# A third fold of the column Fourier transform in an attention and Fourier-mixing kernel, with new step priorities

## The chip, the cores and the metric

The kernel runs on one core of one Trainium2 chip. The metric is the time of one execution on the device, in microseconds (us). Before the change the median of three runs was 578.76 us (578.48 to 579.12). The profile is one execution taken by the hardware profiler. Its lines name the engines: PE (TensorE, the matrix unit; PEld is its weight load), DVE (VectorE), ACT (ScalarE), POOL (GpSimd) and SP (which issues DMAs). L1051 is line 1051 of the kernel before.

## The reference: what is computed

Eight batches of 12 heads, 448 tokens and 64 columns per head go through cosine attention. The result, 448 tokens by 768 columns, goes through the real part of a two-dimensional Fourier transform, a normalisation and a two-layer network:

```python
q_n = q / (norm(q) + 1e-6); k_n = k / (norm(k) + 1e-6)
attn = softmax(q_n @ k_n.T / tau)
x = attn @ v                               # heads side by side: (8, 448, 768)
u = x + real(fft(fft(x, axis=1), axis=2))  # tokens, then columns
un = (u - mean(u)) / sqrt(var(u) + 1e-6)
out = u + relu(un @ w_ch1) @ w_ch2         # 768 -> 3072 -> 768
```

## The kernel before, in words

All steps are put into a list by `Plan.add`: an operation with its name, its engine or the engines that may take it, an estimated duration, a priority, and what it reads and writes. `Plan.schedule` then deals the operations out to the five engines, earliest possible start first and the lower priority number among equals. The result is a fixed order for each engine, which executes its list strictly in that order with semaphore waits between engines. `SHIFT` is a table of corrections, by operation name and occurrence, that are added to the priorities before the scheduling. It holds 335 numbers. So a change in `SHIFT` changes no operation, but it can change the order on each engine and, where two engines are allowed, the engine. `Plan.fill` finally puts short dummy matmuls ("warm" steps, L1571, six matmuls of 128 columns each) where the planner expects PE to be idle.

A batch b goes through these steps (the number after the underscore is the batch, the one before it a part):

- `attn`: for the first two batches `first_norm` squares (`sq`, ACT), sums (`ss`, DVE), takes ln and exp (`ln`, `nrm`, ACT) and a reciprocal (`eps`, `rcp`, DVE) for the norms. It scales (`sc`, L704 and L708, DVE or POOL), transposes with matmuls (`tk` L732, `tq` L744 to L746, `tt` L757) and evacuates PSUM (`ek`, `eq`, `et`, L723 and L767). `tq` writes its 128 results to every third PSUM column. Then come the scores (`qk`, L889, L901, L902), the exponentials (`ex`, L867, ACT), the product with v (`pv`, L920 and L926), a reciprocal and a scaling into `X` (`rd`, `x`, L944 and L946). The pairs of heads are taken in the order 0, 1, 2, 3, 5, 4.
- `fold`, called after the last three pairs: the 448 tokens have been split into sums and differences already. `fa` (L963) and `f0`, `f1` (L970) fold the columns once more; for batches 1 to 7 `g` (L992) folds a second time, into an array `G` of 193 columns by four token parts, for even (eo = 0) and odd (eo = 1) frequencies. `g0` writes columns 1 to 127 after pair 5, `g1` columns 128 to 191 after pair 4; `gc` (L1522, L1523) copies columns 0 and 192. Then the token transform `fs0` (L1013, columns 0 to 127) follows `g0` and `fs1` (columns 128 to 192) follows `g1`. Each is 8 matmuls that move 225 columns, and `te` (L1024 on ACT, L1025 on DVE) evacuates each into `Tt`. For batch 0 the first block is done directly from the first fold (L1008).
- `fft`: the column transform `fd0`, `fd1` (L1051) is 8 matmuls each for batches 1 to 7. They move 193 or 192 columns of the table `CSd` and write contiguous PSUM columns 0 to 192 (even) and 193 to 384 (odd). `qe` (L1064), `pq` (L1067) and `u` (L1079) combine the result with `X`; `ba` (L1111), `bs` (L1113), `ln2` (L1116), `rs` (L1118) and `un` (L1120) normalise. For batch 0 `tn` (L1130) transposes with matmuls and `eu` (L1138) evacuates; for the others a DMA transposes (L1141).
- `ffn`: `h` (L1188) is the first layer, `relu` (L1204) its evacuation, `y` and `m` (L1332) the second layer, `fin` (L1352, L1357, L1364) the addition of u and L1378 or L1386 the store. For the last two batches the first layer runs as a fast product of seven multiplications (`p`, L1283). `wsums` and `sums` prepare sums of weights on DVE.

The network of batch b − 1 and the attention of batch b stand interleaved on PE. In the profile's span the first network step of batch 0, `h0_0`, starts at 51.49 us: what lies before it is called the head here, and the rest the body. The loads of q and k for a batch are issued on SP, those of v and of the weights on POOL.

The tables are made in the head: `sins` and `sind` (L568 to L571) fill `CSs` and `CSd` with ACT's sine, which needs the table loads `ldt0`, `ldt1` and `ldt` (L576, L578, L588); `sinn` (L586) negates a table, and `sinp` (L581) another on POOL.

Of the kernel before, what the change touches and what calls it, by code (L numbers as in the profile page):

```python
# [13 lines left out]
DM = H * DH  # L14
# [8 lines left out]
NG = DM // 4 + 1  # L23
ORDER = (0, 1, 2, 3, 5, 4)
# [54 lines left out]
}  # L79

LATE = {r"W[12]_\d+": 1.5, "tmd": 2.0, r"sq\d_2": 4.0, r"sq\d_\d": 2.0, r"sq[KQT]\d_1": 2.0, r"ktd\d": 3.0, r"qdup\d": 3.0, r"qk\d._[2-7]": 1.5, r"pv\d\d_[2-7]": 2.0, r"pv\d\d_1": 1.0, r"h\d+_[1-7]": 0.3}
PIECE = {r"sc[KQ]\d_0": 0.95, r"scT\d_0": 0.42, r"sc\d_\d": 0.6, r"f[avm]\dp_\d": 0.54, r"t\d\d": 0.94}
PORT = r"eps\d|f[a01]\d_\d|g\d_\d|u\d+_\d|un\d_\d|s\d\d_\d|t\d\d|sc[KQT]\d_\d"

# [318 lines left out]
def t_dve(n, mode=1):  # L408
    return 0.1 + n / (960.0 * mode)
# [1222 lines left out]
```

## Time and profile before

| | us |
|---|---|
| median of 3 runs | 578.76 |
| span of the profiled execution, first to last instruction | 576.7 |
| difference between the two | 2.06 |
| PE busy in the span | 562.2 |
| DVE busy | 428.6 |
| ACT busy | 391.4 |
| POOL busy | 210.7 |

A row of the profile's timeline gives the start, the length, the engine, the line, the operation, what it writes and reads, and how often; in square brackets stands how long the engine was idle before it, and who ended that. In the chain of waits the row gives start, length, and engine with tile and line. Matmuls overlap in a pipeline: one takes 0.2 to 0.3 us from start to end, while the next starts much sooner. So the pace of PE is read from starts, not from durations.

### The profile page before, as it was taken

What the parts mean: (1) busy time and instruction counts of PE and PEld (TensorE: products, weight loads), DVE (VectorE), ACT (ScalarE), POOL (GpSimd) and SP (SyncE); (2) the same over time, 40 slices, a digit from 0 to 9 for tenths busy, and PEclk for the clock granted to TensorE, in tenths of its full rate; (3) what the DMA queues carried; (4) which work ended last, traced back from release to release, by engine and by line L of the source; (5) the groups of instructions that cost most, each with busy time, mean ns of one, the idle gap of its engine ahead of it and who ended that gap; (6) DMA issues with size and microseconds to landing.
All of it is one profiled execution on the core that took longest, in us unless ns stands there. A gap on an engine that the chain in (4) does not pass through costs nothing.

```text
span 576.7 us, 15950 instructions
## 1 busy us (share of the span) xinstructions
PE 562.2 (97%) x6496; PEld 443.3 (77%) x6496; DVE 428.6 (74%) x1066; ACT 391.4 (68%) x764; POOL 210.7 (37%) x323
## 2 busy tenths in 40 slices
PE   3999999999999999999999999999999999999998
PEld 3679888686687786978787687778878687969695
DVE  8879888887688778776768568765877587876363
ACT  8898885467975685687747676488737753848170
POOL 8525424543462525523270435413180120031303
PEclk9899999999999999999999999999999999999999
DMA  9999999892597729952594339932592110022001
GB/s 218 186 218 168 167 180 166 177 166 56 119 150 87 177 44 133 174 110 61 110 140 73 66 103 147 162 70 71 106 108 57 28 57 28 3 42 71 27 30 56
DMA packets 187834, 62.19 MB, mean 108 GB/s; under 512 B 166736, under 2 KB 185552, under 8 KB 187760
## 3 DMA queue, kind: packets, MB, share of 16 engines
q1 hardware_dynamic: 129792, 38.35, 35.2%
q0 software_dynamic: 57968, 22.81, 30.8%
q8 instruction: 51, 0.84, 0.6%
q14 instruction: 23, 0.19, 0.1%
HBM read 51.90 MB, written 11.01 MB: 109 GB/s over the span
## 4 chain that ended last, share of the span: by engine, by line
PE 94%; DVE 3%; POOL 2%; issue 1%; POOLq 0%
PE PS L1332 34%; PE PS L1188 31%; PE PS L1283 7%; PE PS L926 6%; PE PS L889 6%; PE PS L1013 2%; PE PS L920 2%; PE PS L1051 2%; PE PS L744 1%; PE PS L1571 1%; PE PS L901 1%; PE PS L902 1%; POOL VB L847 1%; DVE X L946 1%; DVE SM L679 1%
## 5 line engine op out<-in xcount | busy, mean ns | idle before, releaser
L1188 PE MATMUL PS<-UNT,W1b 128*128 128x256 bf16 (+1 forms) x1872 | 187.9, 256 | 0.0
L1188 PEld LDWEIGHTS PS<-UNT,W1b 128*128 128x128 bf16 x1872 | 156.2, 98 | 18.9 <-issue 4.3
L867 ACT ACTIVATE E<-PS 128x900 bf16<-128x900 f32 (+1 forms) x192 | 148.7, 828 | 27.8 <-PE PS L889 25.7
L1332 PE MATMUL PS<-W2b,HQ 128*128 128x384 bf16 x768 | 133.3, 326 | 0.0
L815 POOL TENSOR_TENSOR QH<-STG,SM 128x256 bf16<-128x256 f32 x126 | 79.1, 655 | 82.1 <-DVE SM L624 73.1
L1332 PEld LDWEIGHTS PS<-W2b,HQ 128*128 128x128 bf16 x768 | 73.9, 98 | 45.4 <-issue 0.9
L1357 POOL TENSOR_TENSOR OUTB<-OUTB,U 128x192 f32<-128x192 f32 x66 | 37.9, 594 | 163.6 <-ACT OUTB L1352 163.3
L1204 ACT ACTIVATE HQ<-PS 128x512 bf16<-128x512 f32 x83 | 49.6, 597 | 42.5 <-PE PS L1188 42.1
L1332 PE MATMUL PS<-TX,HQ 128*128 128x384 bf16 (+2 forms) x408 | 71.0, 321 | 0.0
L1427 DVE TENSOR_TENSOR HQ<-HQ 128x512 bf16<-128x512 bf16 x141 | 60.6, 456 | 13.8 <-ACT HQ L1204 7.7
L1332 PEld LDWEIGHTS PS<-TX,HQ 128*128 128x128 bf16 x408 | 38.4, 98 | 23.5 <-issue 1.1
L926 PE MATMUL PS<-VB,E 128*128 128x65 bf16 x1152 | 51.2, 193 | 0.0
L926 PEld LDWEIGHTS PS<-VB,E 128*128 128x128 bf16 x1152 | 47.6, 97 | 1.1
L806 ACT ACTIVATE QH<-STG 128x384 f32<-128x384 f32 x84 | 42.4, 521 | 7.8 <-DVE SM L808 7.1
L808 DVE TENSOR_REDUCE SM<-QH 128x6 f32<-128x384 f32 x84 | 44.2, 539 | 4.3 <-ACT QH L806 3.9
L1204 DVE TENSOR_SCALAR HQ<-PS 128x512 bf16<-128x512 f32 x43 | 29.7, 691 | 21.1 <-PE PS L1188 20.6
L1386 POOL DMA_INDIRECT out_dram<-OUTB,IDX x21 | 22.9, 1092 | 53.2 <-DVE OUTB L1364 36.4
L920 PE MATMUL PS<-VZ,E 128*128 128x130 bf16 x192 | 41.6, 219 | 0.3 <-DVE X L946 0.3
L889 PE MATMUL PS<-QK 64*128 64x225 bf16 x576 | 39.9, 260 | 0.2 <-ACT E L867 0.2
L1079 DVE SCALAR_TENSOR_TENSOR U<-ACG,X 128x384 bf16<-128x384 f32 (+3 forms) x70 | 39.4, 583 | 0.9
L1352 ACT ACTIVATE OUTB<-PS 128x384 f32<-128x384 f32 x33 | 16.2, 492 | 30.4 <-PE PS L1332 30.1
L946 DVE TENSOR_TENSOR X<-PS,RD 128x512 bf16<-128x512 f32 (+1 forms) x49 | 33.1, 678 | 1.2
(177 smaller groups left out, 795.5 us busy)
## 6 DMA issues: line engine op xcount, KB each, us to landing
STG<-in_k_dram SPq DMA_DIRECT2D x18, 384.0 KB, 4.1
STG<-in_q_dram SPq DMA_DIRECT2D x18, 384.0 KB, 3.8
VB<-in_v_dram POOLq DMA_DIRECT2D x24, 192.0 KB, 5.9
W1b<-in_moe_w_ch_dram POOLq DMA_DIRECT2D x12, 384.0 KB, 6.7
W2b<-in_moe_w_ch_dram POOLq DMA_DIRECT2D x12, 384.0 KB, 7.3
out_dram<-OUTB SPq DMA_DIRECT2D x7, 384.0 KB, 4.0
TX<-in_k_dram SPq DMA_DIRECT2D x2, 576.0 KB, 5.6
TX<-in_q_dram SPq DMA_DIRECT2D x2, 576.0 KB, 6.0
```

Source lines behind the costliest of these rows:

```text
L806: P.add("act", lambda a, sq=sq, src=buf[:, w * x:w * x + w]: a.activation(sq, src, ACTF.Square), t_act(w), pr, f"sq{i}_{b}", reads=bn, wri ...
L808: P.add("dve", lambda v, o=SS[:, i, H // ns * x:H // ns * (x + 1)], sq=sq: v.tensor_reduce(o, sq.rearrange("p (h d) -> p h d", d=DH), AX.X ...
L815: r = v.tensor_tensor(v3(qh)[:, h:h + 4], v3(buf)[:, h:h + 4], RN[:, i, h:h + 4].unsqueeze(2).to_broadcast((128, 4, DH)), AluOp.mult)
L867: return a.activation(o, self.PS[:, bk:bk + nc_, 0:SQ2], ACTF.Exp, scale=1.0 / self.tau)
L889: i = pe.matmul(self.PS[:, bk + h, c0:c0 + NK], self.KT[r, jj, kt * 128:(kt + 1) * 128], self.QT[r, jj, cols], start=True, stop=True)
L920: r = pe.matmul(o, st(6), self.VZ[:, j, :], start=not split, stop=(split and i == 0), skip_group_check=True)
L926: r = pe.matmul(o[:, 65 * h:65 * h + 65], st(2 * kt + h), self.VB[:, kt, 2 * j + h, :], start=(split and i == h == kt == 0), stop=((not sp ...
L1188: r = pe.matmul(self.PS[:, bk, x * n:(x + 1) * n], self.W1b[:, j, ft * 128:(ft + 1) * 128], self.UNT[:, j, cs], start=(j == 0), stop=(j == ...
L1204: return e.activation(o, i, ACTF.Relu) if e is self.nc.scalar else e.tensor_relu(o, i)
L1283: r = pe.matmul(o[:, 128 * f:128 * f + 128], lhs(j, n * g + f), rhs[:, j, :], start=(start and j == 0 and f == 0), stop=(stop and j == 2 a ...
L1332: r = pe.matmul(self.PS[:, bk, 0:n], lhs(f), rhs(f), start=(start and f == 0), stop=(stop and f == NF // 2 - 1), skip_group_check=True)
L1427: P.add("dve", lambda v: v.tensor_tensor(cs(o), cs(a), cs(bq), op), 0.46, -0.5, f"{nm}{k}_{b}", reads=rd, writes=hr(o)(k))
```

## The change

Four things change.

1. `fold`, batches 1 to 7: after `g1`, two new DVE operations `e0` and `e1` fold the even half of `G` a third time, about column 96, into two blocks of 97 columns by four parts (`NM = DM // 8 + 1 = 97`). They lie in the memory of `F`, which is free by then.
2. The token transforms `fs0` and `fs1` of batches 1 to 7 both come after the last fold, in a new function `fsum`. For even frequencies they take the folded blocks (97 columns each instead of 128 and 65). The number of matmuls and the 225 columns moved by each stay. The evacuations still wait for the `pv` of pair 5, the last reader of the memory that they write.
3. `fft`, batches 1 to 7: an even matmul of `fd` moves every second column of the table, 97 or 96 instead of 193, and writes every second PSUM column. The odd ones stay at 192. The number of matmuls stays. Column 96 of the fold would be counted twice, so a new step `halfd` halves one row of the table `CSd` once, after the column transform of batch 0.
4. The table `SHIFT` is replaced as a whole: 446 numbers instead of 335, with 123 operation names in both.

The core of the diff (the `SHIFT` tables and unchanged lines are cut):

```diff
+NM = DM // 8 + 1
...
+        if b and blk:
+            E0 = F[:, 0].rearrange("p a c -> p (a c)")[:, 0:8 * NM].rearrange("p (d a c) -> p d a c", d=2, a=4)
+            for i, o in ((0, AluOp.add), (1, AluOp.subtract)):
+                P.add("dve", lambda v, i=i, o=o: v.tensor_tensor(E0[:, i], G[:, 0, :, 0:NM], gp(G[:], [[NG, 4], [-1, NM]], NG - 1), o), t_dve(4 * NM, 2) + 0.03, pj, f"e{i}_{b}",
+                      reads=["G00", "G01", "G10", "G11", "Gc0", "Gc1"], writes=[f"F0{x}" for x in range(3)] if i == 0 else ["Ed"], after=[P.ops[-1]] if i else [])
+        if b == 0:
+            self.fsum(b, blk, m, direct, pj)
+        elif blk:
+            for x in range(2):
+                self.fsum(b, x, (128, NG - 128)[x], False, pj)
+
+    def fsum(self, b, blk, m, direct, pj):
...
             for eo in range(2):
+                mm = NM if b and eo == 0 else m
                 for s in range(2):
-                    o = self.PS[0:m, bk + eo, s * NK:(s + 1) * NK]
+                    o = self.PS[0:mm, bk + eo, s * NK:(s + 1) * NK]
...
                     for t in range(2):
                         k = 128 if t == 0 else RB
-                        r = pe.matmul(o, G[0:k, eo, 2 * s + t, blk * 128:blk * 128 + m],
-                                      self.CSs[0:k, t, s, :], start=(t == 0), stop=(t == 1))
+                        lhs = E0[0:k, blk, 2 * s + t, :] if b and eo == 0 else G[0:k, eo, 2 * s + t, blk * 128:blk * 128 + m]
+                        r = pe.matmul(o, lhs, self.CSs[0:k, t, s, :], start=(t == 0), stop=(t == 1))
...
-                  writes=[...], after=[tile.users[0], self.pvs[-1 if blk == 0 else -2]], tiles=(tile,))
+                  writes=[...], after=[tile.users[0], self.pvs[-1 if b == 0 and blk == 0 else -2]], tiles=(tile,))
...
+                def mul(c, out, s, eo, d, k, tab, start, stop):
+                    o0 = (2 * eo + d) * SQ2 + s * NK + 128 * kt
+                    return pe.matmul(PS[:, c, out], self.Tt[0:k, o0:o0 + 128], tab, start=start, stop=stop, skip_group_check=True)
                 for d in range(2):
                     k = 128 if d == 0 else NG - 128
                     for s in (1, 0):
+                        if b:
+                            par = d ^ s
+                            mul(bk + s, slice(par, NG, 2), s, 0, d, NM, self.CSd[0:NM, 0, s, par:NG:2], d == 0, False)
+                            r = mul(bk + s, slice(NG, NL), s, 1, d, k, self.CSd[0:k, d, s, NG:NL], False, d == 1)
+                            continue
...
+            if b == 0 and kt:
+                row = self.CSd[NM - 1:NM, 0, :, 0:NG]
+                P.add(("dve", "act"), lambda e: e.activation(row, row, ACTF.Copy, scale=0.5) if e is self.nc.scalar else e.tensor_scalar(row, row, 0.5, None, AluOp.mult),
+                      (0.25, 0.5), 100, "halfd", reads=["CSd"], writes=["CSd"], after=self.fd_ops)
```

More of the change, by code (lines that the diff above doesn't have):

```diff
@@ L995, in fold @@
                   writes=[f"G{blk}{i}"])
+        if b and blk:
[9 more added lines that the diff above has]
+    def fsum(self, b, blk, m, direct, pj):
+        P, F, G = self.P, self.F, self.G
+        FP = DM // 2 + 2
+        E0 = F[:, 0].rearrange("p a c -> p (a c)")[:, 0:8 * NM].rearrange("p (d a c) -> p d a c", d=2, a=4)
         tile = Tile("G")
@@ L1012, in fn @@
                         k = 128 if t == 0 else RB
-                        r = pe.matmul(o, G[0:k, eo, 2 * s + t, blk * 128:blk * 128 + m],
-                                      self.CSs[0:k, t, s, :], start=(t == 0), stop=(t == 1))
+                        lhs = E0[0:k, blk, 2 * s + t, :] if b and eo == 0 else G[0:k, eo, 2 * s + t, blk * 128:blk * 128 + m]
+                        r = pe.matmul(o, lhs, self.CSs[0:k, t, s, :], start=(t == 0), stop=(t == 1))
             return r
         P.add("pe", fn, (16 if direct else 8) * t_mm(NK), pj, f"fs{blk}_{b}",
-              reads=["F00", "F10", "F02", "F12", "CSs", "CSn"] if direct else [f"Gc{blk}", f"G{blk}0", f"G{blk}1", "CSs"], tiles=(tile,), acquire=tile, margin=0.2)
+              reads=["F00", "F10", "F02", "F12", "CSs", "CSn"] if direct else [f"Gc{blk}", f"G{blk}0", f"G{blk}1", "CSs"] + (["F00", "F01", "F02", "Ed"] if b else []), tiles=(tile,), acquire=tile, margin=0.2)
+        me = max(m, NM) if b else m
         for es, ah in ([(("act",), (0,)), (("dve",), (1,))] if b == 0 and blk else [(("act",) if b == 0 else ("act", "dve"), (0, 1))]):
@@ L1020, in ev @@
                 bk, a = self.bank(tile), slice(ah[0], ah[-1] + 1)
-                o = self.Tt[0:m, 0:4 * SQ2].rearrange("p (a d k) -> p d a k", a=2, d=2)[:, blk, a]
-                i = self.PS[0:m, bk + ah[0]:bk + ah[-1] + 1, 0:SQ2]
+                o = self.Tt[0:me, 0:4 * SQ2].rearrange("p (a d k) -> p d a k", a=2, d=2)[:, blk, a]
+                i = self.PS[0:me, bk + ah[0]:bk + ah[-1] + 1, 0:SQ2]
                 if e is self.nc.scalar:
@@ L1027, in fold @@
             P.add(es, ev, [t_act(n_) if e == "act" else t_dve(n_) for e in es], pj, f"te{blk}_{b}",
-                  writes=[f"Tt{blk}" + ("b" if len(ah) == 1 and ah[0] else "")], after=[tile.users[0], self.pvs[-1 if blk == 0 else -2]], tiles=(tile,))
+                  writes=[f"Tt{blk}" + ("b" if len(ah) == 1 and ah[0] else "")], after=[tile.users[0], self.pvs[-1 if b == 0 and blk == 0 else -2]], tiles=(tile,))
     def fft(self, b):
@@ L1046, in fn @@
                     for s in (1, 0):
-                        for eo in range(2):
-                            m0, m1 = (0, 193) if eo == 0 else (193, 385)
-                            o0 = (2 * eo + d) * SQ2 + s * NK + 128 * kt
-                            tab = self.CSd[0:k, d, s, m0:m1] if b or s == 0 or sums[0] == 0 else SP[0:k, d, m0:m1]
-                            r = pe.matmul(PS[:, bk + (s if b else sums[0]), m0:m1], self.Tt[0:k, o0:o0 + 128], tab,
-                                          start=(d == 0 and eo == 0 and (b > 0 or s == 1)), stop=(d == 1 and eo == 1 and (b > 0 or s == 0)),
-                                          skip_group_check=True)
+                        if b:
[3 more added lines that the diff above has]
+                            continue
+                        for eo in range(2):
+                            m0, m1 = (0, NG) if eo == 0 else (NG, NL)
+                            tab = self.CSd[0:k, d, s, m0:m1] if s == 0 or sums[0] == 0 else SP[0:k, d, m0:m1]
+                            r = mul(bk + sums[0], slice(m0, m1), s, eo, d, k, tab, d == 0 and eo == 0 and s == 1, d == 1 and eo == 1 and s == 0)
                 return r
             for sg in (0, 1) if b == 0 else (0,):
-                self.fd_ops.append(P.add("pe", fn if b else lambda pe, fn=fn, sg=sg: fn(pe, sums=(sg,)), 8 * 0.085, pr + 1, f"fd{kt}_{b}",
+                self.fd_ops.append(P.add("pe", fn if b else lambda pe, fn=fn, sg=sg: fn(pe, sums=(sg,)), 8 * (0.085 if b == 0 else 0.064), pr + 1, f"fd{kt}_{b}",
                                          reads=["Tt0", "Tt1", "Tt1b", "CSd"] + (["CSp"] if b == 0 and sg else []),
                                          tiles=(tile,), acquire=None if sg else tile, margin=0.2))
+            if b == 0 and kt:
+                row = self.CSd[NM - 1:NM, 0, :, 0:NG]
+                P.add(("dve", "act"), lambda e: e.activation(row, row, ACTF.Copy, scale=0.5) if e is self.nc.scalar else e.tensor_scalar(row, row, 0.5, None, AluOp.mult),
+                      (0.25, 0.5), 100, "halfd", reads=["CSd"], writes=["CSd"], after=self.fd_ops)
             fds = self.fd_ops[-2:]
```

123 rows, old and new, of the table SHIFT are left out of this document.

## The prediction

> **What bounds the kernel now.** The page comes first.
>
> ```profile
> span 576.7 us, 15950 instructions
> ...
> PE 562.2 (97%) x6496; PEld 443.3 (77%) x6496; DVE 428.6 (74%) x1066; ACT 391.4 (68%) x764; POOL 210.7 (37%) x323
> ...
> PE   3999999999999999999999999999999999999998
> ```
>
> PE is idle for 576.7 − 562.2 = 14.5 us, and the slices put nearly all of it into the first one. The view of stages says the same: 11.75 us of idleness before 51.5 us, none behind it, and 2.9 in the last stage, after the last matmul.
>
> ```profile
> 0.00:51.50 51.50, 39.75 (x576) 32.73 (x577) 43.79 (x103) 45.45 (x72) 29.20 (x53) 0.97 1.25 198
> 51.50:84.00 32.50, 32.50 (x491) 28.34 (x492) 28.58 (x68) 27.58 (x51) 12.17 (x17) 1.00 1.35 173
> ...
> 496.20:576.80 80.60, 77.70 (x922) 61.87 (x919) 47.17 (x112) 40.25 (x82) 16.85 (x28) 1.00 0.14 41
> ```
>
> (The columns are stage, length, then busy time of PE, PEld, DVE, ACT and POOL, clock, DMA.) So there are two terms: the head, until `h0_0`, where ACT and DVE set the pace, and the body, where time is what PE has to do. In the body DVE work is free until a wait reaches PE. The chain of waits shows what ends the head:
>
> ```profile
> 39.70 0.76 DVE F L970 x2
> 40.46 1.26 DVE SM L679
> 41.72 1.05 DVE ACG L992 x2
> ...
> 42.91 0.95 PE PS L1013 x8
> 43.86 1.01 PE PS L1571 x18
> ...
> 44.87 1.53 PE PS L1051 x16
> ...
> 51.49 0.55 PE PS L1188 x7
> ```
>
> The second row matters: a sum for batch 1 (`ssK0_1`) stands on DVE between the first fold of batch 0 and `g1`.
>
> **The change, part by part.** The order on each engine is that of the changed kernel's program; the durations are from rows of before.
>
> *The exponentials of batch 0.* The timeline of the head:
>
> ```profile
> 15.18 1.34 DVE L679 TENSOR_REDUCE SM<-HQ 128x18 f32<-128x1152 f32 x1
> 17.64 0.92 ACT L867 ACTIVATE E<-PS 128x900 bf16<-128x900 f32 x1
> 18.45 0.30 ACT L620 ACTIVATE SM<-SM,MV 128x18 f32<-128x18 f32 x1
> 19.45 0.21 ACT L622 ACTIVATE SM<-SM 128x18 f32<-128x18 f32 x1
> 27.41 0.32 ACT L767 ACTIVATE KTD<-PS 64x192 bf16<-64x192 f32 x1 [0.30 <-PE PS L757]
> 37.01 1.28 ACT L578 ACT_TABLE_LOAD   x1
> 38.30 1.16 ACT L677 ACTIVATE OUTB<-W2b 128x1152 f32<-128x1152 f32 x1
> 39.37 0.93 ACT L568 ACTIVATE CS<-UNT,MV 128x770 bf16<-128x770 f32 x1
> 41.05 1.28 ACT L588 ACT_TABLE_LOAD   x1
> 42.34 0.24 ACT L1522 ACTIVATE ACG<-F 128x8 bf16<-128x8 bf16 x1
> 43.07 1.36 ACT L1024 ACTIVATE E<-PS 128x900 bf16<-128x900 f32 x2
> 44.44 1.15 ACT L677 ACTIVATE W2b<-W2b 128x1152 f32<-128x1152 f32 x1
> 47.66 0.93 ACT L1113 ACTIVATE F<-U,MV 128x768 bf16<-128x768 bf16 x1
> ```
>
> From 17.64 to 37.0 us ACT does little but the 24 exponentials. In the new order one of the two `ln`/`nrm` pairs between them stands ahead of the first, and `et1_0` goes to DVE: 0.30 + 0.21 and 0.32 + 0.30 of waiting leave the stream, 1.13 us. The first exponential now waits for the pair, and so for the sum `ssK1_0` (15.18 to about 16.45). Ahead of that sum DVE gets `sinn` and `scQ2_0` and loses `scK2_0` and `scT2_0`, about as much. 16.45 + 0.51 gives a start near 17.0 instead of 17.64. Together −1.7 us; I take −1.4, since POOL must deliver more of the scalings in time. The bounds are 0 and −1.7.
>
> *From the last exponential to `h0_0`* (37.0 to 51.49, 14.5 us). `g1` comes ahead of `ssK0_1`, which frees 1.26 us of DVE. But ACT now holds a table load (1.28), `gc2`, `sind` (41.05 − 39.37 = 1.68), `sqK0_1` (1.16) and `gc1` (0.24) ahead of `fs1`: 4.65 us, where the trace had 42.91 − 37.0 = 5.9. Between `te1` and the first normalisation `bs0` ACT has `sqT0_1`, the second table load, `sqQ0_1` and a `ln`, 3.2 us, as much as the 47.66 − 44.43 of before. Then `halfd` and `sqK1_1` (1.15) stand ahead of the last evacuations. They partly overlap `un` and `tn`, which costs about 0.5. So 1.25 is won and about 0.75 returned: −0.5 us, bounds +0.2 and −1.2. The cover is thin: a late POOL shows here at once.
>
> *What moves into the body.* The three `tk` of batch 1 (9 matmuls at 1.01 / 18 = 56 ns, 0.5 us) and two more dummy steps (0.34 each) come behind `h0_0`; the three dummy steps of the next-to-last batch go.
>
> ```profile
> 496.24 1.00 PE PS L1571 x18
> ```
>
> ```profile
> 45.21 0.56 DVE L708 TENSOR_TENSOR QH<-W2b,SM 128x384 bf16<-128x384 f32 x1
> ```
>
> That is 0.5 + 0.7 − 1.0 = +0.2 us on PE. `scK0_1` to `scK2_1`, 3 × 0.56 = 1.7 us of DVE, move behind `h0_0` as well. DVE has 32.5 − 28.6 = 3.9 us of room there, and `h` steps lie on PE beside it; I charge +0.3, bounds 0 and +1.7.
>
> *The column transform.* An even matmul moves 97 columns instead of 193, four per `fd`, 14 `fd`: 56 matmuls. The trace has no matmul that writes every second PSUM column and adds to it. The nearest writes every third (L744):
>
> ```profile
> 96.86 1.36 PE PS L1051 x16
> ```
>
> ```profile
> 29.18 0.49 PE L744 MATMUL PS<-TX 128*128 128x128 bf16 x3
> 29.46 0.23 PE L745 MATMUL PS<-TX 128*128 128x64 bf16 x1
> ```
>
> 1.36 / 16 = 85 ns for 192.5 contiguous columns, 0.44 ns each. L744 takes 280 / 3 = 93 ns for 128, 0.73 ns each, where dummy matmuls of the same size take 56. At 0.44 an even matmul costs 43 ns and 56 × 42 = 2.35 us go; at 0.73 it costs 71 and 0.8 us go. At twice the contiguous price it costs 85 and nothing goes. I take −0.8, the row that writes with gaps; bounds 0 and −2.35.
>
> A rule speaks against this part: the Trainium skill ("SBUF — State Buffer", the note on cachelines) says that PSUM has lines of 8 bytes, two fp32 values, so that any non-contiguous pattern significantly slows matmuls. The L744 rows agree. Read strictly, one line for each column, it gives 0 here in place of −0.8, and the sum below would be 577.4.
>
> *The third fold and the later transforms.* `e0` and `e1` work on 388 elements per partition. Rows of L992 lie around them:
>
> ```profile
> L992 DVE TENSOR_TENSOR ACG<-F x30: 236/398/1454, 41.6 to 485.7; 128x256 bf16<-128x256 bf16 x16, 128x508 bf16<-128x508 bf16 x14
> ```
>
> So 0.24 to 0.40 us each, 0.65 per batch, 4.5 in all on an engine that is 74% busy. On PE each `fs` keeps its 8 matmuls, and the evacuations keep their width. What is new is a chain: both `fs` wait for `e1`, then both `te` must end before `fd`, and PE executes in order, so that the whole network queue stands behind a late `fs`. The tightest place is batch 1:
>
> ```profile
> 89.44 0.21 DVE L944 RECIPROCAL RD<-PS 128x8 f32<-128x8 f32 x1 [0.29 <-PE PS L926]
> 92.75 0.18 DVE L1523 COPY ACG<-F 128x8 bf16<-128x8 bf16 x1
> 94.94 1.09 DVE L1025 CAST E<-PS 65x900 bf16<-65x900 f32 x1 [0.70 <-PE PS L1013]
> ```
>
> ```profile
> 87.14 1.31 PE PS L1188 x12
> ...
> 94.90 1.95 PE PS L1332 x12
> ```
>
> From the last `pv` the fold took 92.93 − 89.44 = 3.5 us, with 0.2 of waiting 3.7; `e0`, `e1` make it 4.3. The new order puts five `h` steps (1.31 / 2 = 0.66 each) and three `y` steps (1.95) there, 5.2 us. Batches 2 to 7 have 5.9 to 18 us, counted the same way. Behind the second `fs` there are 1.5 to 2.0 us of PE work before `fd`, as much as before; a `te` ends 0.05 + 1.09 us after its `fs`, and except in batch 2 one is on ACT and one on DVE. So I charge 0, bounds 0 and the rival's price below.
>
> Nothing changes in the queues that counts: on SP the stores and loads keep their order but for neighbours, on POOL the v loads of batch 0 are turned round and one W2 load passes two v loads.
>
> **Sum**, against the profiled execution: −1.4 − 0.5 + 0.2 + 0.3 − 0.8 = −2.2 us, a span of 574.5. The median lies 578.76 − 576.7 = 2.06 above the span, and I carry that over: **576.6 us**.
>
> **Rivals.**
>
> *The head gives nothing.* For it: more of batch 0 hangs on POOL, and 1.26 us freed on DVE only helps if ACT, with its two table loads, is not the end. Against it: the rows of ACT above lose 1.13 us outright. Then the terms are 0 + 0.2 + 0.3 − 0.8: 578.5 us, no change.
>
> *The shorter matmuls are no shorter.* The change doesn't do what it says if 97 columns with gaps cost the 85 ns of 193 without. For it: L744 pays 1.7 times the price per column already, and the new matmuls also add to what stands in PSUM. Against it: L744 writes with a wider gap. The sum is then −1.4, 577.4 us; with a head that gives nothing, 579.3.
>
> *PE waits at `fd`, and it gets slower.* The second `te` decides. If it starts late because DVE or ACT is held by an operation that itself waits (in the new order of batch 3 `te1` stands behind two `eps` that wait for a `nrm` of ACT), `fd` stops PE. The price is up to one evacuation, 1.09 us, in each of 7 batches: 7.6 us, less the 2.2, 584.2 us if all are hit; 580.4 if half are. It decides from a lateness of about 0.5 us per batch, that is 1.64 us of PE cover less 1.14. For it: a DVE that is 74% busy has queues. Against it, from the view of waits:
>
> ```profile
> ACT E L1024 <- PE PS L1013: 8.5, 11, 2.4
> DVE E L1025 <- PE PS L1013: 1.9, 2, 1.2
> ```
>
> ACT and DVE were idle and waiting for `fs` in 13 cases before, so they come early rather than late.
>
> *All of PE's columns count.* Contiguous price for the even matmuls and the whole of the head: −1.7 − 1.2 + 0.2 − 2.35 = −5.0, 573.7 us.
>
> **How the numbers follow.** A measurement of this kernel tells about 0.2%, 1.2 us, from no change. The forecast has 0.35; the same with even matmuls at their full price, 577.4, has 0.15; the best case 0.07; no change, 577.6 to 579.9, 0.20; slower by the wait at `fd` or by a late body 0.23. So faster 0.57, same 0.20, slower 0.23. The range goes from 574.0, short of the best case, to 581.0, which takes in half of the waits at `fd`. The likeliest case's own range is 574.0 to 577.6.
>
> **What would show it.** `h0_0` (the first L1188 or its new line) starts at 49.5 to 50 us instead of 51.49; the last exponential ends near 35.6. Sixteen matmuls of the column transform take 4 × (85 + 71) × 2 = 1.25 us instead of 1.36; 1.02 would mean that the gaps in PSUM are free, 1.36 that they cost double. PE stays at full busy time after `h0_0`, and no wait of PE on L1025, L1024 or the new fold exceeds 0.3 us. I am wrong if the first exponential starts after 17.6, or if PE's list of waits names the evacuations.

## The result, and the profile after

| | before | changed |
|---|---|---|
| median, four runs each on one chip | 578.68 us (578.48 to 579.12) | **581.06 us** (580.75 to 581.55) |
| span of the profiled execution | 576.7 | 579.0 |
| PE / DVE / ACT / POOL busy | 562.2 / 428.6 / 391.4 / 210.7 | 561.3 / 441.3 / 387.4 / 215.7 |

The ratio is 1.0044, 95% interval 1.003 to 1.0059: the changed kernel is **slower**, by 2.4 us. The forecast was 576.6.

The page of the changed kernel:

```profile
span 579.0 us, 15898 instructions
...
PE 561.3 (97%) x6460; PEld 441.5 (76%) x6460; DVE 441.3 (76%) x1085; ACT 387.4 (67%) x757; POOL 215.7 (37%) x326
...
PE   3899999999999999999999999999999999999997
```

PE is busy 0.9 us less and the span is 2.3 us longer. So the loss is waiting on PE, not work, and the slices are too coarse to show where. It has to be read from starts. The timeline of PE, first of the kernel before and then of the changed one, at three points: the first network step (51.49 in the row shown above), the first step of the second layer (`y000_0`), and the last matmuls:

```profile
89.89 0.95 PE L1013 MATMUL PS<-CS,ACG 128*128 128x225 bf16 x8
90.68 2.13 PE L1188 MATMUL PS<-UNT,W1b 128*128 128x256 bf16 x18
92.65 0.98 PE L1332 MATMUL PS<-W2b,TX 128*128 128x384 bf16 x5
...
572.74 1.16 PE L1332 MATMUL PS<-TX,HQ 128*128 128x256 bf16 x15
```

```profile
49.89 0.49 PE L1247 MATMUL PS<-UNT,W1b 128*128 128x128 bf16 x6 [0.34 <-ACT UNT L1197]
...
93.02 2.11 PE L1391 MATMUL PS<-W2b,TX 128*128 128x384 bf16 x12
...
574.83 1.05 PE L1391 MATMUL PS<-TX,HQ 128*128 128x256 bf16 x14
```

The first step starts 1.6 us earlier, `y000_0` 0.4 later, the last matmul ends 2.0 later (575.88 against 573.90). The token transform `fs0` of batch 1 stood ahead of `y000_0` in the kernel before (90.68 − 89.89 = 0.79 us) and stands behind it now. Taken out, the stage from `h0_0` to `y000_0` took 92.65 − 51.49 − 0.79 = 40.37 us and now takes 93.02 − 49.89 = 43.13: **2.76 us more**, more than the head had won. Its matmuls are the same but for the nine transposes (`tk`) and the two dummy steps that moved in, 1.2 us by the prediction's count; the rest is waiting.

The second place is the token transforms. In the changed kernel's chain of waits around batch 2 (start, length, engine, tile and line) DVE holds PE up with the folds `f`, `g1` (L1024) and the new `e` (L1031):

```profile
168.21 1.48 DVE F L1002 x2
169.71 1.46 DVE ACG L1024 x2
171.27 0.87 DVE F L1031 x2
172.28 1.76 PE PS L1063 x16
174.03 1.97 PE PS L1247 x18
176.00 1.34 PE PS L1096 x16
```

Its PE timeline at that point and at batch 4:

```profile
170.84 0.82 PE L1247 MATMUL PS<-UNT,W1b 128*128 128x256 bf16 x6
172.28 0.57 PE L1063 MATMUL PS<-CS,F 128*97 128x225 bf16 x4 [0.62 <-DVE F L1031]
...
300.43 0.60 PE L1063 MATMUL PS<-CS,F 128*97 128x225 bf16 x4 [0.48 <-DVE F L1031]
```

A network step takes 1.97 / 3 = 0.66 us, and the next matmul came 172.28 − 170.84 = 1.44 after that start: 0.78 lost. The same reading gives 0.65 in batch 4. **1.43 us** together, at the place where the prediction charged nothing.

The third is the column transform, which did not get shorter: the last row of the chain has 1.34 us for its sixteen matmuls, where the kernel before had 1.36.

### The profile page after: what moved, and what is told of

Its sections match the earlier page's. It is cut to its first block, busy times and chain, and to the rows that moved or that the text cites. A ratio compares the mean times of both kernels' runs of the same rounds, so it can differ in the third digit from the quotient of the medians.

```text
span 579.0 us, 15898 instructions
## 1 busy us (share of the span) xinstructions
PE 561.3 (97%) x6460; PEld 441.5 (76%) x6460; DVE 441.3 (76%) x1085; ACT 387.4 (67%) x757; POOL 215.7 (37%) x326
## 4 chain that ended last, share of the span: by engine, by line
PE 89%; DVE 6%; ACT 2%; issue 1%; POOL 1%; POOLq 0%; DVEq 0%
PE PS L1391 34%; PE PS L1247 28%; PE PS L1342 7%; PE PS L958 6%; PE PS L921 5%; PE PS L1063 2%; PE PS L952 2%; PE PS L1096 2%; DVE ACG L1024 1%; PE PS L933 1%; ACT E L899 1%; DVE SM L711 1%; PE PS L934 1%; DVE F L1002 1%; PE PS L776 1%
## 5 line engine op out<-in xcount | busy, mean ns | idle before, releaser
L1486 DVE TENSOR_TENSOR HQ<-HQ 128x512 bf16<-128x512 bf16 x141 | 60.9, 459 | 10.3 <-PE PS L1391 5.7
L958 PE MATMUL PS<-VB,E 128*128 128x65 bf16 x1152 | 51.2, 193 | 0.0
L840 DVE TENSOR_REDUCE SM<-QH 128x6 f32<-128x384 f32 x84 | 43.9, 539 | 8.5 <-ACT QH L838 8.3
L1423 DVE TENSOR_TENSOR OUTB<-PS,OUTB 128x384 f32<-128x384 f32 x33 | 18.3, 553 | 22.9 <-PE PS L1391 21.5
```

Source lines behind the costliest of these rows:

```text
L840: P.add("dve", lambda v, o=SS[:, i, H // ns * x:H // ns * (x + 1)], sq=sq: v.tensor_reduce(o, sq.rearrange("p (h d) -> p h d", d=DH), AX.X ...
L958: r = pe.matmul(o[:, 65 * h:65 * h + 65], st(2 * kt + h), self.VB[:, kt, 2 * j + h, :], start=(split and i == h == kt == 0), stop=((not sp ...
L1486: P.add("dve", lambda v: v.tensor_tensor(cs(o), cs(a), cs(bq), op), 0.46, -0.5, f"{nm}{k}_{b}", reads=rd, writes=hr(o)(k))
```

## The experiments

Each kernel is the changed one with one edit unless said otherwise, compared with the kernel before on the same chip, which took 578.5 to 578.8 us on all of them. The changed kernel's 581.06 is from the chip of the result; differences of tenths of a us are read from the traces. The diffs are shortened to the lines that matter, and operations stand in them by their names.

| kernel | median us | ratio to before (95%) |
|---|---|---|
| contiguous PSUM, wrong columns | 579.24 | 1.0005 (0.9997 to 1.0014) |
| POOL's scalings held | 579.78 | 1.0016 (1.0008 to 1.0025) |
| old transform, new order | 579.45 | 1.0010 (0.9994 to 1.0026) |
| scalings of batch 1 put back | 582.31 | 1.0063 (1.0051 to 1.0075) |
| no dummy steps in the body | 580.75 | 1.0041 (1.0029 to 1.0053) |
| evacuations back to ACT | 581.63 | 1.0053 (1.0040 to 1.0066) |
| blocks of 97 columns | 579.51 | 1.0014 (1.0002 to 1.0026) |
| blocks + POOL held | 577.80 | 0.9981 (0.9967 to 0.9994) |
| order of before to the second `h0_0` | 581.54 | 1.0035 (1.0015 to 1.0056) |
| the same, three repairs | 578.74 | 0.9985 (0.9966 to 1.0005) |
| the same, buffers renamed | 580.81 | 1.0037 (1.0024 to 1.0050) |
| the same, three repairs | 578.38 | 0.9995 (0.9985 to 1.0006) |
| order of before to the end of batch 1's attention | 579.50 | 1.0012 (1.0003 to 1.0021) |
| the same, three repairs | **576.23** | **0.9951 (0.9938 to 0.9965)** |

### Contiguous PSUM

```diff
-mul(bk + s, slice(par, NG, 2), s, 0, d, NM, ...)
+mul(bk + s, slice(0, NM) if par == 0 else slice(NM, NG), s, 0, d, NM, ...)
```

> The changed kernel with one edit: an even matmul of the column transform still moves 97 or 96 columns, taken as every second one of the table, but writes them side by side into PSUM instead of into every second column. The even frequencies so land in wrong columns of the output; all else, the order included, is as it was. Theory A (the gaps in PSUM are what costs): the two starts of an even and the next odd matmul, 168 ns in the changed kernel, come to about 43 + 85 = 128 ns; 56 pairs of 40 ns are 2.2 us, so about 578.8 us instead of 581.06. Rival (the strided reading of the table, the weight load or a least time of a matmul costs): the pair stays near 168 ns and the time at 581.

579.24 us, 1.8 less. The groups by form of the changed kernel (busy, mean ns of one) and of this one, and this one's chain:

```profile
L1096 PE MATMUL PS<-CS,E 65*128 65x192 bf16 x34 | 7.6, 276 | 0.0
...
L1096 PE MATMUL PS<-CS,E 97*128 97x96 bf16 x28 | 6.5, 248 | 0.0
```

```profile
L1096 PE MATMUL PS<-CS,E 65*128 65x192 bf16 x34 | 6.6, 248 | 0.0
L1096 PE MATMUL PS<-CS,E 97*128 97x96 bf16 x28 | 5.5, 210 | 0.0
```

```profile
175.93 1.07 PE PS L1096 x16
```

1.07 against 1.34 for sixteen: a pair takes 134 ns instead of 168. By starts, the even matmul was followed after 50 ns and the odd one after 118 in the changed kernel; now 49 and 85. So the gap in the writing costs 34 ns per pair, and it falls on the *next* matmul, whose rows here grow from 248 to 276 ns. Theory A holds (134 rather than the 128 expected: 97 columns take 49 ns, not 43). Whether the other 6 ns are the price of reading every second column of the table is not shown.

### POOL's scalings held

```diff
+pick("pool", "sc5_3").deps.add(pick("dve", "e1_2"))
+pick("pool", "sc5_5").deps.add(pick("dve", "e1_4"))
```

Why is `g1` late in two batches only? Two operations of 0.28 us (0.50 for both in the rows below) take 1.45 and 2.50 there. The timelines of DVE and of POOL in the changed kernel:

```profile
169.71 1.45 DVE L1024 TENSOR_TENSOR ACG<-F 128x256 bf16<-128x256 bf16 x2
...
297.21 2.50 DVE L1024 TENSOR_TENSOR ACG<-F 128x256 bf16<-128x256 bf16 x2
```

```profile
168.37 0.71 POOL L881 DMA_DIRECT2D VZ<-in_v_dram  x1
...
169.72 1.91 POOL L847 TENSOR_TENSOR QH<-STG,SM 128x256 bf16<-128x256 f32 x3
...
297.76 1.78 POOL L847 TENSOR_TENSOR QH<-STG,SM 128x256 bf16<-128x256 f32 x3
```

> The changed kernel, but POOL's scaling for the next batch that ran beside the fold g1 of batch 2 and of batch 4 waits for the third fold (e1) of that batch. Theory B (DVE's fold stands while POOL runs its two-operand scaling): the second g1 of batch 2 takes about 0.28 us instead of 1.2 and that of batch 4 0.28 instead of 2.29; PE's waits ahead of the first token transform of these batches, 0.78 and 0.65 us, go, and the time falls by about 1.4 us to 579.6. Rival (the third fold, two operations of 0.36 us, is itself what makes the token transform late): the g1 rows stay long or the waits shrink by less than half, and the time stays above 580.5.

579.78 us, 1.3 less. DVE's rows in this kernel:

```profile
168.03 0.43 DVE L1486 TENSOR_TENSOR HQ<-HQ 128x512 bf16<-128x512 bf16 x1 [0.22 <-ACT HQ L1263]
...
169.16 0.76 DVE L1002 TENSOR_TENSOR F<-ACG 128x512 bf16<-128x512 bf16 x2
169.96 0.51 DVE L1024 TENSOR_TENSOR ACG<-F 128x256 bf16<-128x256 bf16 x2
170.78 0.64 DVE L1031 TENSOR_TENSOR F<-ACG 128x388 bf16<-128x388 bf16 x2 [0.31 <-ACT ACG L1581]
...
172.25 0.77 DVE L1486 TENSOR_TENSOR HQ<-HQ 128x512 bf16<-128x512 bf16 x1
...
297.18 0.50 DVE L1024 TENSOR_TENSOR ACG<-F 128x256 bf16<-128x256 bf16 x2
```

Both pairs of `g1` are short again, the fold `f` ahead of them in batch 2 too (0.76 instead of 1.48), and no wait of PE on L1031 is left in the view of waits. So POOL's scalings are what made the folds late, and in that Theory B holds. In batch 2 both operations of `g1` were slow (0.83 and 0.70 us; the expectation's 1.2 is no single row), in batch 4 only the second (2.29). The Trainium skill ("SBUF — State Buffer", the section on the two sides of SBUF) has a rule for it: a DVE operation with two inputs in SBUF and a GpSimd operation that reads SBUF share one pair of ports, which is an exclusive lock and not a shared bandwidth. The ends of the rows agree: the two `g1` of batch 2 end 0.16 us after the first and the second scaling, the slow one of batch 4 ends 0.17 us after the third.

The starts do not agree. The slow `g1` of batch 4 begins 0.34 us ahead of the first scaling's row, and `f` of batch 2 was slow wholly ahead of it (168.21 to 169.68), beside rows in which POOL issues loads of v (L881 above). With the scalings held, such a row lies beside `f` too (169.32), and `f` is fast. How a scaling holds a fold ahead of its own row, or whether its row begins too late in the profile, stays open.

### The old transform in the new order

```diff
-mm = NM if b and eo == 0 else m
+mm = m
...
-lhs = E0[0:k, blk, 2 * s + t, :] if b and eo == 0 else G[...]
+lhs = G[...]
...
+gone = [o for o in self.P.ops if o.name == "halfd" or re.fullmatch(r"e[01]_[1-7]", o.name)]
```

and the column transform of the kernel before.

> The changed kernel's order on every engine, but with the old transform: no third fold, token transforms from the second fold with 128 and 65 columns, column transform with 193 contiguous columns, no halving of the row. Both token transforms still stand where the new order has them. Theory A + B: the column transform costs the same 168 ns a pair, so nothing is lost there; the 0.64 us of the third fold come off the waits of batches 2 and 4 (0.78 and 0.65 us), which leaves about 0.15: 579.8 us. What the prediction held (the shorter matmuls save 0.8 and the fold costs nothing): 581.9. If the third fold were the whole loss: 578.7 or less.

579.45 us, 1.6 less. In batches 2 and 4 the token transform follows the start of the network step ahead after 0.66 and 0.65 us, so the whole 1.43 us of waiting is gone. `g1` of batch 2 is as slow as ever (DVE, then PE):

```profile
169.82 1.45 DVE L1024 TENSOR_TENSOR ACG<-F 128x256 bf16<-128x256 bf16 x2
```

```profile
171.59 1.65 PE L1063 MATMUL PS<-CS,ACG 128*65 128x225 bf16 x15
```

But without the 0.64 us of `e` behind it the token transform is just in time: no idle time stands in its row. So the wait needs both, the stall by POOL and the longer chain: with either one removed it goes. With its gaps in PSUM the third fold cost 1.4 us and saved 0.1.

### The first scalings of batch 1 put back

```diff
+move("dve", [rcp1, scK0_1, scK1_1, scK2_1], before=un0_0)
+move("act", [ek0_1, ek1_1, ek2_1], before=eu01_0)
+move("pe", [tk0_1, tk1_1, tk2_1], before=tn0_0)
```

The dummy steps behind the transposes wait for the evacuations, and the waits for PSUM buffers follow the new order.

> The changed kernel, with the first three scalings of batch 1 on DVE, their transposes on PE and their evacuations on ACT put back ahead of the first normalisation of batch 0, where the kernel before had them. Theory C (DVE is full from the last exponential to about 62 us, so that work moved behind the first network step is only moved): the first network step starts 1.5 to 2 us later than 49.9, the next occurrence of it (64.0 us) stays within 0.4, and the time stays within 0.4 of 581.06. What the prediction held (the head's gain is real, the moved work costs 0.8 of it): 581.06 + 1.6 - 0.8 = 581.9 or more.

582.31 us, 1.25 more. The first network step starts at 52.38, 2.5 later, and the stage to its second occurrence takes 13.2 us instead of 14.1. Theory C falls: this move does pay. What the new order loses there lies elsewhere.

### No dummy steps in the body

```diff
+i = [o.name for o in L].index("h0_0")
+order["pe"] = L[:i] + [o for o in L[i:] if o.name != "warm" or o.start > 100.0]
```

> The changed kernel without the three dummy steps that stand behind the first network step, between 51.5 and 58 us (18 matmuls, 1.0 us of PE; the kernel before has one there). Theory E (they stand where PE would wait anyway): waits take their place and the time stays within 0.4 of 581.06. Rival (they hold PE up, since the planner put them where the chip has no idle time): 0.7 to 1.0 us less, 580.1 to 580.4.

580.75 us: within the interval of the changed kernel. Where the three dummy steps stood, the timeline of PE now has

```profile
52.59 0.33 PE L764 MATMUL PS<-TX,QH 128*128 128x128 bf16 x3 [0.61 <-ACT TX L1263]
...
58.59 0.49 PE L776 MATMUL PS<-TX 128*128 128x128 bf16 x3 [0.73 <-ACT QK L755]
```

Theory E holds: the stage from `h0_0` to `y000_0` takes 43.14 us, as with the dummy steps. (What the profile gains lies elsewhere: its token transform of batch 4 does not wait.) A dummy step hides a wait from the view of waits: PE has some 1.0 us more of idle time at this point than that view admits.

### Evacuations back to ACT

```diff
+to_act("eq2_1", before="et0_1")
+to_act("eu20_0", before="ex0_1", k=1)
+to_act("eu21_0", before="ex0_1", k=1)
```

> The changed kernel, with three evacuations that the new order gives to DVE between 59 and 62 us (eq2 of batch 1 and the two eu2 of batch 0, 0.63 + 1.02 us) given back to ACT, which had them before. Theory D (between the first and the second occurrence of the first network step DVE is the late engine: 15.4 us of its work, overlaps counted, in 14.1 us): that stage becomes 0.6 to 1.0 us shorter and the time 580.1 to 580.5. Rival (ACT is as full there, 12 of 14 us, and the exponentials of batch 1 come later instead): no change within 0.4, or slower.

581.63 us, 0.6 more. The evacuations now lie between the exponentials (timeline of ACT), and PE waits for them at the next scores (timeline of PE):

```profile
62.10 0.85 ACT L1197 ACTIVATE UNT<-PS 128x384 bf16<-128x384 f32 x2
62.84 0.91 ACT L899 ACTIVATE E<-PS 128x900 bf16<-128x900 f32 x1
```

```profile
63.01 0.56 PE L921 MATMUL PS<-QK 64*128 64x225 bf16 x8 [0.48 <-ACT UNT L1197]
```

Theory D falls in this form: load moved from one full engine to the other only changes who is late.

### Contiguous blocks, in the right place

```diff
-SN[sg], PS[:, bank, 0:NL], SN[2]
+gp(SN[sg], [[2 * NM, 2], [1, 2], [2, NM]]), PS[:, bank, 0:4 * NM] as (e a q), SN[2] as (e a q)
```

with the odd matmul writing two blocks as well and `u` reading at the new offsets.

> The changed kernel with contiguous writes of the column transform that still end in the right place: even and odd frequencies each stand in PSUM as two blocks of 97 columns (every second frequency in a block), and the subtraction and addition on DVE (pq) write them interleaved into SBUF; 388 columns instead of 385. Theory A: the pair of an even and an odd matmul at 134 ns as with contiguous writes alone, and 579.2 us. Rival (the interleaved writing by DVE, or the odd matmul that now reads every second column, gives part of it back): 579.8 to 581.

579.51 us. Interleaving in `pq` costs nothing (groups of DVE, the changed kernel and this one: busy, mean ns):

```profile
L1126 DVE TENSOR_TENSOR ACG<-PS,ACG 128x385 f32<-128x385 f32 x28 | 14.9, 554 | 4.5 <-ACT ACG L1123 3.8 <-PE PS L1391 0.5 <-ACT SM L654 0.2
```

```profile
L1128 DVE TENSOR_TENSOR ACG<-PS,ACG 128x388 f32<-128x388 f32 x28 | 15.0, 556 | 3.4 <-PE PS L1104 2.5 <-ACT ACG L1125 0.5
```

The odd matmul, which reads every second column and writes two blocks, takes 90 to 93 ns instead of 85, so a pair has 140 and not 134; which of the two costs this is not shown. Most of the 1.8 us stays.

### Blocks and POOL held together

Both edits above in one kernel.

> The blocks of 97 columns and, besides, POOL's two scalings held until the third folds of batches 2 and 4 have ended. If the two causes are separate, the gains add: 581.06 - 1.8 - 1.3 = 577.9 us, 0.15% under the kernel before. If the shorter column transform only uncovers the next wait: 579.

577.80 us, 3.26 less. Alone the two edits gave 1.55 and 1.28, 2.83 together, so neither takes anything from the other: the two causes are separate. Its span is 575.9 us. This version is already a little faster than the kernel before.

### Where the head's gain goes: the order of before up to a seam

For the 2.76 us the order itself was tried: every engine runs the list of the kernel before up to a point, the seam, then the rest of the new list (the graft, in the expectations).

```diff
+for e in engines:
+    order[e] = first[e] + [o for o in order[e] if o not in done]
```

> The changed kernel, in which every engine works through the order of the kernel before, its dummy steps included, up to the second occurrence of the first network step, and then through the rest of the new order. Theory F (the new order of the head and the start of batch 1 gives back by that point what it won: 64.03 us against 63.46): the first h0_0 starts at 51.5 and the second at 63.5 again, and the time is 0.3 to 0.7 lower, 580.4 to 580.8. What the prediction held (the new head is worth 1.9 and costs 0.5 behind it): 1.4 us slower, 582.5. A third case: the new order had prepared more of batch 1 by then, so that the gain at 63.5 is lost by the first fold: 581.

> The same graft with the blocks of 97 columns and POOL's two scalings held, that is all three repairs in one kernel. If they add: 577.8 - 0.5 = 577.3 us, 0.25% under the kernel before. If the graft brings nothing: 577.8.

581.54 and 578.74 us: inconclusive, since at the seam the second `h0_0` took a PSUM buffer that was still in use, and PE waited 1.2 us for it. With the buffers behind the seam renamed:

> The graft again, with the PSUM buffers behind the seam renamed, so that each new tile takes the buffer that has been free longest. In the first graft the second h0_0 took the buffer of h20_0 and waited 1.2 us for its evacuation, a wait of the seam itself. Theory F: the second h0_0 starts near 63.4, and the time is 0.3 to 0.7 under the changed kernel, 580.4 to 580.8. Third case (the new order had prepared more of batch 1 by then): the gain at 63.4 is lost in waits before the first fold of batch 1, and the time stays at 581. What the prediction held: 582.5.

> The mended graft with the blocks of 97 columns and POOL's two scalings held. If the three add: 577.3 us, 0.25% under the kernel before; if the graft brings nothing: 577.8.

580.81 and 578.38 us; the second is slower than both of its forecasts. In the first, the second `h0_0` now starts at 62.84, 1.2 us before that of the changed kernel, yet `y000_0` at 93.12 as ever. The lead is lost a step further on, at the scores that the new order asks for at once (PE, this kernel):

```profile
64.73 0.56 PE L1014 MATMUL PS<-QK 64*128 64x225 bf16 x8 [1.08 <-ACT E L992]
```

By the time alone Theory F and the third case can't be told apart; by `y000_0` the third case held, and the question became whether the rest of batch 1's attention loses it in the new order or in any. The seam was put behind that attention:

> The graft with a later seam: every engine works through the order of the kernel before up to the end of batch 1's attention (the step ahead of its first token transform), and then through the rest of the new order. Theory G (the new order of batch 1's attention, from the second h0_0 to y000_0, loses what the head won: 29.0 us there against 28.4 without the token transform before): y000_0 starts at 91.9 instead of 93.0, and the time is 1.1 us under the changed kernel, 580.0. Rival (the lead is lost again in the third fold of batch 1, or whatever the order): y000_0 at 93, or fs0_1 waits, and 581.

> The same graft with the blocks of 97 columns and POOL's two scalings held. If the three add: 577.8 - 1.1 = 576.7 us, 0.35% under the kernel before. If the graft brings nothing: 577.8.

579.50 and 576.23 us. PE in the first of these:

```profile
50.83 1.33 PE L1348 MATMUL PS<-UNT,W1b 128*128 128x128 bf16 x21
...
91.27 2.11 PE L1492 MATMUL PS<-W2b,TX 128*128 128x384 bf16 x12
```

91.27 − 50.83 = 40.44 us, the 40.37 of before. Theory G holds: the new order from the first network step to the end of batch 1's attention is what cost the 2.76 us. The seam puts the old head back with it, so whether the new head can be had with the old order behind it was not tried. How the new order cost time shows in the chains of waits. That of the changed kernel leaves PE for ACT at 51.6 and for DVE at 55.2, while that of this kernel stays on PE but for the transposes' inputs at 55 to 57:

```profile
51.60 0.61 ACT TX L1263
...
55.23 0.87 DVE F L1179
...
56.13 0.69 DVE TX L1263
...
58.08 1.26 DVE SM L711
...
59.80 0.62 DVE QK L755
```

```profile
50.83 4.19 PE PS L1348 x72
...
60.23 1.34 PE PS L1348 x24
```

Ahead of the evacuation at 59.80, which PE needs for the transposes and scores of batch 1, the new order has a normalisation, a `relu` and a sum of 1.26 us on DVE. Which of them would have to go elsewhere was not tried one by one and stays open; two guesses (scalings put back, evacuations to ACT) were wrong.

The last kernel has all three repairs, and beats both:

```profile
span 575.0 us, 15933 instructions
```

## Why the prediction was wrong, step by step

| step of the sum | forecast | measured | how |
|---|---|---|---|
| head, to `h0_0` | −1.9 | −1.6 | 49.89 against 51.49 |
| first step to `y000_0`: transposes 0.5, dummy steps 0.7, scalings 0.3 | +1.5 | +2.8 | 43.13 against 40.37 |
| three dummy steps at 496 us gone | −1.0 | −1.0 | no such row is left |
| column transform | −0.8 | −0.1 | 1.34 against 1.36 us, seven times |
| third fold, later token transforms | 0 | +1.4 | waits of batches 2 and 4 |
| after the last matmul | 0 | +0.3 | 3.12 against 2.80 us |
| the rest, not traced | 0 | +0.5 | what is missing to 2.3 |
| span | −2.2 | +2.3 | |

*The head* was right in sum, and its parts partly offset each other. The exponentials end at 36.5 instead of 35.6, so 0.5 us came there and not 1.4; from there to `h0_0` it is 13.4 us, so 1.1 came there and not 0.5. The timeline of ACT:

```profile
17.53 0.90 ACT L899 ACTIVATE E<-PS 128x900 bf16<-128x900 f32 x1
...
32.74 3.75 ACT L899 ACTIVATE E<-PS 128x450 bf16<-128x450 f32 x5
36.51 1.28 ACT L610 ACT_TABLE_LOAD   x1
```

One profile is a rough measure here: among the eight profiles with the new head unchanged `h0_0` starts at 49.4 to 50.8, among the seven with that of before at 50.8 to 51.9. By the medians, 50.0 and 51.2, the head is worth 1.2 us.

*The column transform* is the step where the mechanism failed. The prediction priced the gap in PSUM by L744, 0.73 ns per column, because it was the nearest row. But 0.73 is the mean of three matmuls that do not cost the same. By their starts in the trace they take 64, 109 and 109 ns: the first stands behind a matmul that writes without gaps, and the price falls on the matmul behind. 109 ns for 128 columns is 0.85 ns each; 97 columns at that price cost 83 ns instead of 85, and 0.1 us go, as measured. The same answer lay in the rule that the prediction quoted against itself: the Trainium skill ("SBUF — State Buffer", the note on cachelines) read strictly gave 0, and 0.1 came. The test named in advance decided it: 1.36 us would mean that the gaps cost double, and 1.34 were measured.

*The third fold at nothing.* The prediction named the token transforms as the place where a late chain stops PE, but it counted cover in durations of an undisturbed DVE: 0.65 us for `e0`, `e1`, and 5.9 us or more of PE work to cover a chain of 4.3 in batches 2 to 7. In batch 2 `f`, `g1` and `e` took 1.48 + 1.46 + 0.87 = 3.8 us, where they take 0.76 + 0.51 + 0.64 = 1.9 undisturbed (the rows of DVE with POOL held). From the last `pv` to the end of `e`, counted as in the prediction, the chain of batch 2 took 6.3 us (165.80 to 172.13), and 4.7 with POOL held. The prediction had looked at POOL's queue for DMAs only, not at what POOL computes beside the fold. Yet its own row of L992 held the sign: it took the shortest and the middle of 236/398/1454 ns and passed over the longest. That one is a `g1` of batch 6 in the kernel before (420.61 us), beside two additions of POOL (L1357); it ends 0.17 us after the second, and there PE did not wait. The rows that were to show no wait of PE on the new fold above 0.3 us show 0.62 and 0.48. Of the two signs that were to show the prediction wrong neither came: the first exponential starts at 17.53, and PE's list of waits names no evacuation `te`. So the wait at `fd`, the rival that was to make it slower, did not occur; the slowing came one step earlier on the same chain.

*The move into the body* is where a size was off: 2.8 instead of 1.5. The matmuls moved (0.5) were counted right. The dummy steps (0.7) were counted as work, but without them PE waits there instead, so of the 2.8 some 2.3 are waiting. "DVE has 3.9 us of room" is an average over a stage; its order decides, and there a sum of 1.26 us stands ahead of an evacuation that PE needs. Since the head is worth 1.2 to 1.6 us and this costs 2.8, the new order of head and batch 1 loses 1.2 to 1.6, and the seam behind it returned 1.6 (581.06 to 579.50).

## What to carry to other kernels

Here a matmul that wrote every second PSUM column cost as much as one that wrote all of them; the interleaving belongs into the evacuation, where it was free. A new link in a chain has to be priced with what runs beside it on the other engines (here POOL), not with its own duration, and the longest row of a group is worth a look before its middle is used. Where an order is replaced as a whole, a gain ahead of a point counts only if the milestones behind it move as well. When many things change at once, keeping the order on every engine fixed and undoing one part (or the reverse, old order up to a seam) separates causes that a new plan would mix.

## What was not expected of the hardware

- The price of the gaps in PSUM falls on the matmul behind: starts follow after 50 ns for the one with gaps, and after 118 instead of 85 for the next, which writes contiguously. A price read from the rows of the writing matmul alone would have been zero.
- A pair of folds on DVE took 2.50 us instead of 0.50 beside three scalings of POOL (1.78 us in all): in batch 4 DVE did not get in between two of them, in batch 2 it did. In the kernel with POOL held, the stall only moved: beside the same scalings, in the row below, an addition on DVE (L1486 at 172.25) took 0.77 us instead of 0.43, but PE did not wait for it. The price of these cases ranged from 0.34 to 2.0 us; what decides its size is open.

```profile
171.56 1.94 POOL L847 TENSOR_TENSOR QH<-STG,SM 128x256 bf16<-128x256 f32 x3 [0.87 <-ACT KTD L1581]
```

- The start of the first network step varies by 1.4 us between profiles of the same head, while the stage from there to `y000_0` took 43.1 to 43.9 us in all of them.
